# Probabilities transposed in half-height tiles, query blocks paired two apart, value products stacked

## The chip, the cores and the metric

The kernel runs on one core of a Trainium2 chip. The metric is the device time of one execution in microseconds. Three runs of the kernel before took 336.01, 339.49 and 340.27 us, so their median is 339.49 us; the profiled execution is a fourth one.

## The reference

Causal attention with a window of 128 keys and a slope per head (8 batches, 8 heads, 576 tokens, 64 numbers per head), and then a mixture of 8 experts in which each token goes to its best expert and each expert keeps its 80 tokens with the highest gate:

```
scores = scale * np.matmul(q, k.transpose(0, 1, 3, 2))
bias = slopes[:, None, None] * (-np.abs(rel).astype(np.float32))[None, :, :]
mask = (rel >= 0) & (rel < window)
scores = np.where(mask, scores + bias[None], -1000000000.0)
attn = softmax(scores)
x = np.matmul(attn, v)            # then (B, S, H * D): 4608 rows of 512
logits = x @ w_gate
expert_idx = np.argmax(logits, axis=1)
for e in range(E):
    tok_idx = the 80 tokens of expert e with the largest gate_w
    h = np.maximum(x[tok_idx] @ w1[e], 0.0)
    out[tok_idx] = gate_w[tok_idx, None] * (h @ w2[e])
```

All other rows of the output are zero.

## The kernel before

**The attention** takes some two thirds of the time. Queries are cut into 9 blocks of 64 rows (t = 0 to 8), heads into 4 pairs (g = 0 to 3). A block of queries sees three blocks of keys: its own (role 2) and the two before it (roles 1 and 0); for t = 0 the first two don't exist. A unit is a set of two neighbouring blocks of one pair of heads, (g, t) and (g, t+1), or two pairs at t = 8; there are 18 units in a batch. A cycle does two units, so a batch has 9 cycles and the whole attention 72. In each cycle TensorE does, in this order:

- `turned`, twice: the masked scores `e` of a unit (128 partitions: 2 blocks of 64 queries; 3 roles of 2 heads times 64 keys) are turned by three 128x128 transposes into a PSUM bank `pt`, and one `Exp` on ScalarE writes them as `ptb`, the keys of one head in partitions 0 to 63 and of the other in 64 to 127.
- `attend`, for each of two earlier units: 12 products `av<-v,ptb` (2 heads, 2 blocks, 3 roles) of 64 rows and 64 columns of weights with 73 moving columns (64 of v, 8 of gate logits and a one), each in a quadrant of the 128x128 array. The results of six units stand side by side in the two banks `av`; `attended` copies them into `xs` on ScalarE only after the sixth.
- `scores`, after each `attend`: 4 quadrant products `s<-kp,q` of 192 columns for the unit two cycles on. VectorE adds the bias and takes the row minimum (`e`, `mn`); GpSimd, for one of the four pieces ScalarE, subtracts it.

A float32 product in a quadrant is two records of TensorE in the trace, and a transpose is one; each has its own load of weights (PEld).

**Side work** goes between the scores of a cycle and the next cycle's transposes (`sides`): the gate logits of the values (`value_logits`: `s<-l_vt,wg`), their transposes into the columns of v (`value_columns`: `s<-ident,lxb` and the copies `v<-s` on VectorE), and the steps that merge each batch's best 80 tokens (`ttt`, `ts`, `at`).

**Order.** A planner records all operations of the attention with costs (`_cost`) and writes each engine's order out; `strict` keeps the three TensorE parts of a cycle in the order of the loop. Engines run in that order and wait on semaphores. SyncE issues the loads and stores in order; `transfers` says which go with which cycle, and a `None` in its lists is filled with one of the stores of zeros to the output (36 of 256 KB). Each is paced by a mark, a transpose's `Exp` or a score's reduction.

**The experts** follow the attention's merge: from 238 to 327 us, with weights that are loaded at the same time. The change does not touch them.

Of the kernel before, what the change touches and what calls it, by code (L numbers as in the profile page):

```python
# [29 lines left out]
class Plan:  # L30
# [107 lines left out]
    def add(self, ns_name, eng, name, args, kw):  # L138
# [12 lines left out]
        if name == "transpose":  # L151
            cols = 256.0 if outs[0].dtype == F32 else 128.0
        elif name == "matmul":
            cols = self._free(kw["rhs"]) * self._free(kw["lhsT"]) / P * (4 if kw["rhs"].dtype == F32 else 1)
# [8 lines left out]
        else:  # L163
# [4 lines left out]
            if name == "transpose" and not op.full:  # L168
                op.tiled = 2
# [61 lines left out]
    def pace(self, call, lead):  # L231
        call.leads.append(lead)
        call.op.deps.setdefault(lead.op, False)
# [152 lines left out]
def tile_attention_then_moe(  # L386
# [55 lines left out]
    def spare(i, k=0):  # L442
        return sps[i % 2][k][:, 128 if i < NUN and units[i][1][0][1] == 0 else 192:512]

# [18 lines left out]
    bn0 = const.tile([P, H, 128], F32, name="bn0")  # L463
# [11 lines left out]
    def make_bias(g):  # L475
        for h in (2 * g, 2 * g + 1):
            add_bias(bn0[:, h], h, ALL, rel0)
        for h in (2 * g, 2 * g + 1):
            add_bias(bneg[:, h], h, ALL, rel)
# [9 lines left out]
    kps = [persist.tile([P, 64 + S], F32, name=f"kp{i}") for i in range(NQ)]  # L489
    for rows in (LOW, HIGH):  # L490
        nc.gpsimd.iota(rel_i[rows], pattern=[[-1, 192]], base=WIN, channel_multiplier=1)
    nc.gpsimd.memset(kps[0][:, 0:64], 0.0)
# [3 lines left out]
    nc.vector.tensor_copy(rel0, rel[:, 64:192])  # L496
    nc.vector.memset(rel0[0:64, 0:64], FAR)
    make_bias(0)

    qs, v_t = {}, {}  # L500

    vts = [persist.tile([P, NP, NKB, VW], F32, name=f"v{i}") for i in range(2)]
    vtt = {}

    def load_v(b, g):
        w = NKB * VW
        return nc.sync.dma_start(
            out=vts[b % 2][:, g].rearrange("p n c -> p (n c)"), in_=v[b][:, w * g:w * g + w])
# [6 lines left out]
    def load_k(b, g, a=0, c=S):  # L515
        return nc.sync.dma_start(out=kps[(b * NP + g) % NQ][:, 64 + a:64 + c], in_=k[b, g, :, a:c])
# [6 lines left out]
    def load_pair(b, g):  # L523
        for a, c in ((0, 256), (256, S)) if b + g == 0 else ((0, S),):
            load_k(b, g, a, c)
            load_q(b, g, a, c)

    load_pair(0, 0)
    wg = const.tile([P, NP, 32], F32, name="wg")
    nc.sync.dma_start(out=wg.rearrange("p g c -> p (g c)"), in_=w_gate)  # L530
    for g in range(2):
        load_vt(0, g)
    load_pair(0, 1)
    for g in range(2):
        load_v(0, g)
    for g in range(2, NP):
        load_vt(0, g)
    load_pair(0, 2)
    load_pair(0, 3)
    for g in range(2, NP):  # L540
        load_v(0, g)
# [4 lines left out]
    for t in kps[1:]:  # L546
        nc.gpsimd.memset(t[:, 0:64], 0.0)
# [30 lines left out]

    def selection_constants():
# [19 lines left out]
        nc.gpsimd.iota(bi, pattern=[[S, B], [P, NU]], base=P, channel_multiplier=0)  # L599
# [83 lines left out]
    def lay(b, bank, gs, us, hh, par):  # L683
        rows, of = (LOW, HIGH)[hh], (LOW, HIGH)[par]
        u0, u1 = us
        lv = bank[:, 0:32 * (gs[1] - gs[0]) * (u1 - u0)].rearrange("p (u g c) -> p g u c", u=u1 - u0, c=32)
        k1 = min(2 * u1, NKB)
        nc.vector.tensor_copy(
            vts[b % 2][rows, gs[0]:gs[1], 2 * u0 + par:k1:2, D:VW],
            lv[of, :, 0:(k1 - 2 * u0 - par + 1) // 2, 9 * hh:9 * hh + 9])  # L690

    def value_columns(b, bank, us, gs=(0, NP)):
# [8 lines left out]
        for hh in range(2):  # L701
            for par in range(2):
                lay(b, bank, gs, us, hh, par)

    def blocks(g, t):
        return (g, t), (g, t + 1)

    BATCH = [blocks(g, t) for g in (0, 1) for t in (0, 2, 4)]
    BATCH += [blocks(g, 6) for g in range(NP)] + [((2 * u, 8), (2 * u + 1, 8)) for u in range(2)]
    BATCH += [blocks(g, t) for g in (2, 3) for t in (0, 2, 4)]  # L710
    NB = len(BATCH)
    NUN = B * NB
    units = [(i // NB, BATCH[i % NB]) for i in range(NUN)]
    es, pts, marks = {}, {}, {}

    def scores(i):
        b, st = units[i]
        (g, t), (g2, _) = st
        e = work.tile([P, 3, 2, 64], F32, tag="e", name=f"e{i}", bufs=6)
        mn = small.tile([P, 2], F32, tag="mneg", name=f"mn{i}", bufs=6)  # L720
        es[i] = e
        sp = sps[i % 2]
        o0 = 64 if t == 0 else 0
        n = 192 - o0
        with nc.together():
            for hh in range(2):
                for j, (gg, t_) in enumerate(st):
                    hs = slice(64 * hh, 64 * hh + 64)
                    nc.tensor.matmul(
                        sp[hh][64 * j:64 * j + 64, 0:n],  # L730
                        lhsT=qs[b, gg][hs, 64 * t_:64 * t_ + 64],
                        rhs=kps[(b * NP + gg) % NQ][hs, 64 * (t_ - 1) + o0:64 * (t_ - 1) + 192],
                        start=True, stop=True)
        yield
        for hh in range(2):
            bias = bnx[:, g // 2, hh] if g != g2 else bn0[:, 2 * g + hh] if t == 0 else bneg[:, 2 * g + hh]
            m = mn[:, hh:hh + 1]
            x = e[:, o0 // 64:, hh]
            marks["s", i] = nc.vector.tensor_tensor_reduce(
                x, sp[hh][:, 0:n].rearrange("p (k c) -> p k c", c=64),  # L740
# [636 lines left out]
```

## Time and profile before

| what | value |
|---|---|
| runs | 336.01, 339.49, 340.27 us; median 339.49 |
| profiled execution | 335.38 us, its span 333.6 us |
| TensorE busy, matrix products | 310.1 us, 93% of the span |
| VectorE, ScalarE, GpSimd busy | 56%, 45%, 39% |
| instructions | 16,416 |
| attention | from about 5 to 220 us |

The span is the time from the first to the last instruction; the execution's own time has 1.8 us around it. Busy shares are means over the whole span, and attention and experts differ: in the attention VectorE is above 80% and TensorE at 99%. A record of TensorE is as long as its data takes to go through, and records overlap, so what one costs is read from the distance between the starts of neighbours.

### The profile page before, as it was taken

What the parts mean: (1) busy time and instruction counts of PE and PEld (TensorE: products, weight loads), DVE (VectorE), ACT (ScalarE), POOL (GpSimd) and SP (SyncE); (2) the same over time, 40 slices, a digit from 0 to 9 for tenths busy, and PEclk for the clock granted to TensorE, in tenths of its full rate; (3) what the DMA queues carried; (4) which work ended last, traced back from release to release, by engine and by line L of the source; (5) the groups of instructions that cost most, each with busy time, mean ns of one, the idle gap of its engine ahead of it and who ended that gap; (6) DMA issues with size and microseconds to landing.
All of it is one profiled execution on the core that took longest, in us unless ns stands there. A gap on an engine that the chain in (4) does not pass through costs nothing. (4 is left out here: it accounts for less than half of the span.)

```text
span 333.6 us, 16416 instructions
## 1 busy us (share of the span) xinstructions
PE 310.1 (93%) x6727; PEld 226.4 (68%) x6727; DVE 187.2 (56%) x1005; ACT 151.1 (45%) x392; POOL 129.3 (39%) x351
## 2 busy tenths in 40 slices
PE   7998998999998999999899999998779999999992
PEld 5585766777776777777686787786675566655560
DVE  7665766787896797887697789775101011110000
ACT  8464555645654645655456556532003322223221
POOL 8543563464463455455346448400710111011111
PEclk9999999999999999999999999999759999999998
DMA  7989999999999899999889888971599999999300
GB/s 216 385 276 360 318 300 269 333 320 323 317 325 313 279 340 292 349 335 310 274 281 301 252 269 283 330 269 40 170 292 392 393 394 402 398 395 398 101 22 21
DMA packets 45131, 97.07 MB, mean 291 GB/s; under 512 B 4864, under 2 KB 5504, under 8 KB 45056
## 3 DMA queue, kind: packets, MB, share of 16 engines
q1 hardware_dynamic: 44032, 93.21, 81.5%
q0 software_dynamic: 1024, 2.81, 2.8%
q8 instruction: 53, 0.87, 1.1%
q14 instruction: 22, 0.18, 0.1%
HBM read 74.19 MB, written 21.81 MB: 288 GB/s over the span
## 5 line engine op out<-in xcount | busy, mean ns | idle before, releaser
L352 POOL TENSOR_SCALAR e<-e,mn 128x192 f32<-128x192 f32 (+1 forms) x216 | 88.0, 415 | 89.6 <-DVE mn L352 78.6
L352 PE MATMUL av<-v,ptb 64*64 64x73 f32 x3072 | 87.2, 228 | 5.4 <-issue 3.9
L352 ACT ACTIVATE ptb<-pt 128x256 f32<-128x256 f32 (+1 forms) x144 | 62.0, 463 | 59.5 <-PE pt L352 58.3
L352 PEld LDWEIGHTS av<-v,ptb 64*64 64x64 f32 x3072 | 73.2, 132 | 20.8 <-issue 15.6
L352 PE MATMUL s<-kp,q 64*64 64x192 f32 (+1 forms) x1152 | 78.2, 314 | 1.2 <-DVE mn L352 0.8
L352 DVE CUSTOM_DVE_ANT_0 e<-s,bneg 128x192 f32<-128x192 f32 x192 | 62.1, 352 | 30.2 <-PE s L352 27.5
L352 PE MATMUL pt<-ident,e 128*128 128x128 f32 x400 | 59.3, 281 | 1.5 <-POOL ij L352 0.8
L352 PEld LDWEIGHTS pt<-ident,e 128*128 128x128 f32 x400 | 43.1, 140 | 12.0 <-issue 3.7
L1328 DVE TENSOR_TENSOR ys<-ys,y 80x512 f32<-80x512 f32 x8 | 5.5, 684 | 80.5 <-ACT ys L1323 80.5
L1296 PEld LDWEIGHTS h<-xgTs,w 128*64 128x64 f32 x1024 | 39.6, 145 | 9.8 <-issue 9.3
L1296 PE MATMUL h<-xgTs,w 128*64 128x80 f32 x1024 | 41.4, 243 | 3.2 <-issue 2.7
L1321 PE MATMUL y<-w,hT 128*32 128x512 f32 (+1 forms) x288 | 42.8, 594 | 0.0
L352 PEld LDWEIGHTS s<-kp,q 64*64 64x64 f32 x1152 | 39.2, 132 | 3.6 <-issue 2.1
L352 ACT ACTIVATE e<-e,mn 128x192 f32<-128x192 f32 (+1 forms) x72 | 31.7, 440 | 18.3 <-DVE mn L352 18.3
L1272 POOL DMA_INDIRECT out_dram<-ys,sid x8 | 7.4, 920 | 79.0 <-ACT hT L1301 73.8
L352 ACT COPY xs<-av 128x438 f32<-128x438 f32 (+2 forms) x79 | 28.5, 401 | 15.2 <-PE av L352 14.2
L1321 PEld LDWEIGHTS y<-w,hT 128*32 128x32 f32 (+1 forms) x288 | 10.5, 105 | 25.0 <-issue 24.2
L352 DVE DVE_READ_ACCUMULATOR2_ANT mn<- 128x1 f32 x288 | 23.9, 83 | 0.0
L352 DVE TENSOR_SCALAR_CACHE_REDUCE ncm<-s 128x272 bf16<-128x272 f32 (+8 forms) x69 | 22.8, 380 | 1.3 <-PE s L352 1.3
L1301 ACT ACTIVATE hT<-h 128x320 f32<-128x320 f32 x16 | 7.0, 437 | 36.1 <-PE h L1296 36.1
L352 DVE CUSTOM_DVE_ANT_0 e<-s,bn 128x128 f32<-128x128 f32 x64 | 16.6, 289 | 12.0 <-PE s L352 10.2
L1321 PE MATMUL yx_d<-w,hT 128*32 128x512 f32 x32 | 15.2, 598 | 0.0
(149 smaller groups left out, 323.8 us busy)
## 6 DMA issues: line engine op xcount, KB each, us to landing
w<-in_moe_w_dram SPq DMA_DIRECT2D x48, 512.0 KB, 11.0
v<-in_v_dram SPq DMA_DIRECT2D x32, 328.5 KB, 4.8
x_dram<-xs SPq DMA_DIRECT2D x32, 292.0 KB, 4.8
l_vt<-in_vt_dram SPq DMA_DIRECT2D x32, 288.0 KB, 4.7
out_dram<-zero SPq DMA_DIRECT2D x36, 256.0 KB, 4.5
kp<-in_k_dram SPq DMA_DIRECT2D x31, 288.0 KB, 4.5
q<-in_q_dram SPq DMA_DIRECT2D x31, 288.0 KB, 4.8
w<-in_moe_w_dram SPq DMA_DIRECT2D x32, 256.0 KB, 4.2
```

What stands on the lines that cost most here:

```text
L352: c.ins = c.f(*c.args, **c.kw)
L1272: put = nc.gpsimd.indirect_dma_start(out=out, out_offset=bass.IndirectOffsetOnAxis(ap=sid[:, e:e + 1], axis=0), in_=ys, in_offset=None, bo ...
L1296: nc.tensor.matmul(hp[64 * hh:64 * hh + 64, R * fi:R * fi + R], lhsT=a[:, cc, f0:f0 + 64], rhs=xgT[:, cc], start=(cc == 0), stop=(cc == NC ...
L1301: relu = nc.scalar.activation(hT[:, 4 * f2:4 * f2 + 4].rearrange("p c r -> p (c r)"), hp[:, 0:4 * R], AF.Relu)
L1321: nc.tensor.matmul(o, lhsT=hT[:, f_, l0:l1], rhs=c[:, f_], start=st, stop=sp)
L1328: nc.vector.tensor_tensor(ys, ys, yp[0:R, 0:DM], ALU.add)
```

## The change

- **Pairs.** A cycle is written as a pair of two sets x = 0 and 1, and a set now holds blocks two apart, (g, t) and (g, t+2), or both pairs of heads at the same t, or blocks 0 and 1. The two sets of a pair mostly hold t and t+1, so that in the order (set, role) two neighbouring roles are two neighbouring key blocks, which a 128-row tile of v can hold.
- **Transposes.** `turned` does a whole cycle: for each head and each 128 columns of `e`, one transpose for rows 0 to 63 and one for rows 64 to 127, that is 12 of 64 rows of weights by 128 columns with 64 moving columns. The two row halves go to the two banks `pt`, alternating. There are still two `Exp` a cycle.
- **Products.** `attend` does a whole cycle: first 8 products with 128 rows of weights (two key blocks stacked) and 64 columns, then 8 quadrant products with 64 rows for the remaining block of each set (4 where only one set has one).
- **Copies.** The results stand in columns 0 to 145 of the two `av` banks in every cycle and are copied out in every cycle: 22 copies a batch in place of 8.
- **Transfers.** v is stored in HBM with 128 rows by all heads (five loads a batch, the last with 64 rows, for four, with the same bytes), x leaves in nine stores of 64 rows a batch in place of five of 128 or 64 (`SLOT` says which blocks share a tile). k and q are loaded earlier in the batch. The copies `v<-s` are six a batch in place of eight, and the columns of v are made in cycles 4 and 8 of the batch before.
- Ten `iota` in place of one, smaller first bias tables, and the planner's costs of half-height transposes.

```diff
@@ costs of the planner
-                return 109.0 if outs[0].dtype == F32 else 55.0
+                return 55.0 if outs[0].dtype != F32 else 109.0 if ins[0].shape[0] > 64 else 34.0
...
-            if name == "transpose" and not op.full:
+            if name == "transpose" and op.full and ins[0].shape[0] <= 64:
+                op.tiled, op.full = 1, False
+            elif name == "transpose" and not op.full:
                 op.tiled = 2
...
+    SLOT = ((3, 5), (2, 4), (6, 8), (0, 1), (7,))
...
+    def two(g, t):
+        return (g, t), (g, t + 2)
...
+    BATCH = [
+        (two(0, 2), two(0, 3)), (two(1, 2), two(1, 3)), (both(0, 0), both(0, 1)),
+        (two(0, 6), both(0, 7)), (two(1, 6), two(2, 3)), (two(2, 2), two(3, 3)),
+        (two(3, 2), both(2, 7)), (two(2, 6), first(2)), (two(3, 6), first(3)),
+    ]
...
+    def turned(c):
+        e = es.pop(c)
+        full, thirds = parts_of(c)
+        pt = work.tile([P, 2, 2, 3, 64], F32, tag="ptb", name=f"ptb{c}", bufs=2)
+        pts[c] = pt
+        i0 = 0 if full else 1
+        banks = [p_[:, 0:384].rearrange("p (h i q) -> p h i q", h=2, i=3) for p_ in ptp]
         with nc.together():
...
+            for hh in range(2):
+                cols = e[:, hh].rearrange("p x r c -> p (x r c)")
+                for i in range(i0, 3):
+                    w = 64 if i == 1 and not thirds else P
+                    for j, rows in enumerate((LOW, HIGH)):
+                        nc.tensor.transpose(
+                            banks[j][0:w, hh, i], cols[rows, P * i:P * i + w], ident[rows, rows])
+        for j in range(2):
+            marks["t", c, j] = nc.scalar.activation(
+                pt[:, j, :, i0:].rearrange("p h i q -> p h (i q)"),
+                banks[j][:, :, i0:].rearrange("p h i q -> p h (i q)"), AF.Exp)
...
+        with nc.together():
+            for x in range(0 if full else 1, 2):
                 for hh in range(2):
...
+                    for j, (g, t) in enumerate(pair[x]):
+                        product(x, hh, j, pt[:, j, hh, 2 * x], V[:, (t - 1) // 2 if t else 0, 2 * g + hh], hh == 0)
+        with nc.together():
+            for hh in range(2):
+                for j in range(2):
+                    for x in range(2 if thirds else 1):
+                        g, t = pair[x][j]
+                        rows, kb = (HIGH, t - 2) if x else (LOW, t)
+                        product(x, hh, j, pt[rows, j, hh, 1], V[rows, kb // 2, 2 * g + hh], not full and not x and hh == 0)
+        attended(c)
...
+            for of, u, rows, g in lot:
+                (nc.vector.tensor_copy if last and x else nc.scalar.copy)(
+                    xsb[b % 2][rows, u, 2 * g:2 * g + 2].rearrange("p h c -> p (h c)"), avp[x][of, 0:2 * VW])
...
+                2: vt_[0:1], 3: vt_[1:4], 4: [k_[0], q_[0], v_[0]], 5: [v_[1], k_[1], q_[1]],
+                6: v_[2:5], 7: [k_[2], q_[2], k_[3]],
...
     for c in range(1, NCY):
...
+        strict(turned, c)
...
+        strict(attend, c - 1)
+        if c + 2 < NCY:
+            scored(c + 2, 0)
...
+            scored(c + 2, 1, list(sides(c)))
...
-    for u in range(3):
+    for u in range(1, NU):
         store_x(LAST, u)
```

TensorE's order in the middle of the attention before, from the transposes of a full cycle to the second half of its scores (a row is a product or a transpose, `x2` are two of them; `pt_79` and `pt_80` are the banks of the transposes, `av_85` and `av_86` those of the value products):

```order
L352 MATMUL pt_79<-ident,e_493 128x128 x3
L352 MATMUL pt_80<-ident,e_496 128x128 x3
L352 MATMUL av_85<-v_97,ptb_498 64x73 x2
L352 MATMUL av_86<-v_97,ptb_498 64x73 x2
L352 MATMUL av_85<-v_97,ptb_498 64x73 x2
L352 MATMUL av_86<-v_97,ptb_498 64x73 x2
L352 MATMUL av_85<-v_97,ptb_498 64x73 x2
L352 MATMUL av_86<-v_97,ptb_498 64x73 x2
L352 MATMUL s_0_81<-kp_93,q_0_479 64x192 x2
L352 MATMUL s_1_82<-kp_93,q_0_479 64x192 x2
```

And a full cycle there now, from the last transposes to the first scores (in the rows `x4` eight stacked products, in the single ones the eight quadrants):

```order
L355 MATMUL pt_79<-ident,e_309 128x64
L355 MATMUL pt_80<-ident,e_309 128x64
L355 MATMUL av_85<-v_98,ptb_311 64x73 x4
L355 MATMUL av_86<-v_98,ptb_311 64x73 x4
L355 MATMUL av_85<-v_98,ptb_311 64x73
L355 MATMUL av_86<-v_98,ptb_311 64x73
...
L355 MATMUL s_0_81<-kp_93,q_0_298 64x192 x2
L355 MATMUL s_1_82<-kp_93,q_0_298 64x192 x2
L355 MATMUL s_0_83<-kp_93,q_0_298 64x192 x2
L355 MATMUL s_1_84<-kp_93,q_0_298 64x192 x2
```

The two stretches of products of a cycle now stand one behind the other with two tile shapes, and the transposes alternate between the banks.

ScalarE's order in two cycles of the middle before (`ptb<-pt` are the exponentials, `e<-e,mn` the fourth piece's subtraction):

```order
L352 ACTIVATE ptb_475<-pt_79 128x384
L352 ACTIVATE ptb_476<-pt_80 128x384
L352 ACTIVATE e_472<-e_472,mn_473 128x3x64
L352 ACTIVATE e_480<-e_480,mn_481 128x3x64
L352 ACTIVATE ptb_484<-pt_79 128x384
L352 ACTIVATE ptb_485<-pt_80 128x384
```

And two cycles now:

```order
L355 ACTIVATE ptb_369<-pt_79 128x384
L355 ACTIVATE e_366<-e_366,mn_367 128x192
L355 ACTIVATE ptb_369<-pt_80 128x384
L355 COPY xs_125<-av_85 128x146
L355 COPY xs_125<-av_86 128x146
L355 ACTIVATE ptb_373<-pt_79 128x384
L355 ACTIVATE e_371<-e_371,mn_372 128x192
L355 ACTIVATE ptb_373<-pt_80 128x384
L355 COPY xs_125<-av_85 128x146
L355 COPY xs_125<-av_86 128x146
```

Two copies have come into each cycle, behind its second exponential.

SyncE's order in the first batch before, from the last first loads to the next batch's gate inputs `l_vt_154`:

```order
L352 DMA v_97<-in_v_dram 128x657 x2
L352 DMA out_dram<-zero 128x512
L352 DMA l_vt_154<-in_vt_dram 128x576
L352 DMA out_dram<-zero 128x512 x3
L352 DMA l_vt_154<-in_vt_dram 128x576
L352 DMA out_dram<-zero 128x512
L352 DMA l_vt_154<-in_vt_dram 128x576 x2
```

And now, with `l_vt_143` for the same inputs:

```order
L355 DMA kp_96<-in_k_dram 128x576
L355 DMA q_3_104<-in_q_dram 128x576
L355 DMA out_dram<-zero 128x512 x10
L355 DMA l_vt_143<-in_vt_dram 128x576
L355 DMA out_dram<-zero 128x512 x2
L355 DMA l_vt_143<-in_vt_dram 128x576 x3
```

Twelve stores of zeros, in place of five, stand ahead of the last three loads of `l_vt`.

## Rows read from the trace of the kernel before

**Rows 1.** Page, busy time of each engine (share of the span) and instructions.
```profile
PE 310.1 (93%) x6727; PEld 226.4 (68%) x6727; DVE 187.2 (56%) x1005; ACT 151.1 (45%) x392; POOL 129.3 (39%) x351
```

**Rows 2.** Windows: length, busy us (instructions) by engine, granted clock, DMA share, GB/s.
```profile
60.00:80.00 20.00, 19.83 (x507) 15.38 (x506) 16.57 (x90) 10.78 (x27) 10.36 (x29) 1.00 0.96 324
```

**Rows 3.** Waits of TensorE and its loads: us in total, times, longest.
```profile
PE av L352 <- issue: 3.9, 7, 1.5
...
PEld av L352 <- ACT xs L352: 2.4, 9, 0.3
```

**Rows 4.** Timeline of TensorE's products in one cycle: start, length of the stretch.
```profile
17.34 0.32 PE L352 MATMUL s<-kp,q 64*64 64x192 f32 x1
...
17.48 0.50 PE L352 MATMUL s<-kp,q 64*64 64x192 f32 x6
17.91 0.51 PE L352 MATMUL s<-ident,lxb 64*128 64x64 f32 x5
18.35 0.87 PE L352 MATMUL pt<-ident,e 128*128 128x128 f32 x6
19.16 0.61 PE L352 MATMUL av<-v,ptb 64*64 64x73 f32 x24
19.59 0.51 PE L352 MATMUL s<-kp,q 64*64 64x192 f32 x8
19.91 0.56 PE L352 MATMUL av<-v,ptb 64*64 64x73 f32 x24
20.30 0.50 PE L352 MATMUL s<-kp,q 64*64 64x192 f32 x8
20.73 0.88 PE L352 MATMUL pt<-ident,e 128*128 128x128 f32 x6
```

**Rows 5.** The av banks' instructions: duration in ns, least, median, most; first and last start.
```profile
L352 PE MATMUL av<-v,ptb x3072: 220/223/276, 13.1 to 220.2; 64*64 64x73 f32 x192
L352 PE MATMUL av<-ident,lxb x5: 216/222/273, 11.4 to 11.7; 64*128 64x64 f32 x4, 64*64 64x64 f32 x1
```

**Rows 6.** Timeline of TensorE among the experts.
```profile
254.78 0.60 PE L1321 MATMUL y<-w,hT 128*32 128x512 f32 x3
...
255.21 0.60 PE L1321 MATMUL y<-w,hT 128*32 128x512 f32 x3
...
255.75 4.65 PE L1296 MATMUL h<-xgTs,w 128*64 128x80 f32 x128
260.33 0.49 PE L1254 MATMUL xgT<-ident,xn 80*128 80x80 f32 x4
```

**Rows 7.** ScalarE's groups from 60 to 200 us: busy us, mean ns.
```profile
L352 ACT ACTIVATE ptb<-pt 128x384 f32<-128x384 f32 x74 | 34.6, 487 | 30.5 <-PE pt L352 29.4
L352 ACT ACTIVATE e<-e,mn 128x192 f32<-128x192 f32 x37 | 16.7, 453 | 6.4 <-DVE mn L352 6.4
L352 ACT COPY xs<-av 128x438 f32<-128x438 f32 x22 | 10.5, 529 | 4.7 <-PE av L352 4.1
L352 ACT COPY xs<-av 64x146 f32<-64x146 f32 x20 | 5.5, 276 | 0.1
L352 ACT COPY xs<-av 128x292 f32<-128x292 f32 x10 | 4.0, 404 | 3.0 <-PE av L352 2.8
```

**Rows 8.** Timeline of TensorE in the first batch, with a stall.
```profile
26.87 0.30 PE L352 MATMUL av<-v,ptb 64*64 64x73 f32 x7
28.63 0.49 PE L352 MATMUL av<-v,ptb 64*64 64x73 f32 x17 [1.46 <-issue]
28.93 0.51 PE L352 MATMUL s<-kp,q 64*64 64x192 f32 x8
29.37 0.45 PE L352 MATMUL s<-l_vt,wg 128*32 128x288 f32 x4
```

**Rows 9.** Timeline of SyncE's queue: start and length of issues.
```profile
17.21 1.68 SPq L352 DMA_DIRECT2D out_dram<-zero  x3
...
21.41 0.87 SPq L352 DMA_DIRECT2D l_vt<-in_vt_dram  x2
```

**Rows 10.** Windows of the first batch, columns as in Rows 2.
```profile
14.00:16.00 2.00, 2.00 (x36) 1.00 (x29) 1.19 (x7) 0.23 (x1) 0.83 (x2) 1.00 1.03 391
16.00:18.00 2.00, 2.00 (x58) 1.54 (x57) 1.67 (x8) 1.21 (x3) 0.53 (x2) 1.00 0.72 247
22.00:24.00 2.00, 2.00 (x68) 1.55 (x60) 1.16 (x8) 0.94 (x3) 1.02 (x3) 1.00 0.94 239
```

**Rows 11.** DMA issues: KB of each, median us from issue to landing.
```profile
l_vt<-in_vt_dram SPq DMA_DIRECT2D x32, 288.0 KB, 4.7
out_dram<-zero SPq DMA_DIRECT2D x36, 256.0 KB, 4.5
```

More of the change, by code (lines that the diff above doesn't have):

```diff
@@ L598, in selection_constants @@
         bi = const.tile([P, B, NU], I32, name="bi")
-        nc.gpsimd.iota(bi, pattern=[[S, B], [P, NU]], base=P, channel_multiplier=0)
+        for j, rows in enumerate((LOW, HIGH)):
+            for u in range(NU):
+                at_ = SLOT[u][min(j, len(SLOT[u]) - 1)] - j
+                nc.gpsimd.iota(bi[rows, :, u], pattern=[[S, B]], base=P + 64 * at_, channel_multiplier=0)
         nc.vector.tensor_copy(idc[:, :, 0], bi.rearrange("p b u -> p (b u)"))
@@ L700, in value_columns @@
         yield
[L701 to L724, printed above, removed]
+        for u0, u1, rw in ((us[0], min(us[1], NU - 1), ALL), (NU - 1, us[1], LOW)):
+            for hh in range(2 if u0 < u1 else 0):
+                lv = bank[rw, n * (u0 - us[0]):n * (u1 - us[0])].rearrange("p (u g c) -> p u g c", u=u1 - u0, c=32)
+                nc.vector.tensor_copy(
+                    vts[b % 2][rw, u0:u1, 2 * gs[0] + hh:2 * gs[1]:2, D:VW], lv[:, :, :, 9 * hh:9 * hh + 9])
@@ new lines, in tile_attention_then_moe, with scores @@
+    units = [tuple(first_role(x, st) for x, st in enumerate(p_)) for p_ in BATCH]
+    units = [(c // CB, units[c % CB], BATCH[c % CB]) for c in range(NCY)]
+    es, mns, pts, marks = {}, {}, {}, {}
+    def scores(c, x):
+        b, r0, st = units[c][0], units[c][1][x], units[c][2][x]
+        if x == 0:
+            es[c] = work.tile([P, 2, 2, 3, 64], F32, tag="e", name=f"e{c}", bufs=3)
+            mns[c] = small.tile([P, 2, 2], F32, tag="mneg", name=f"mn{c}", bufs=3)
+        e, mn, sp = es[c], mns[c], sps[x]
+        n = 192 - 64 * r0
@@ L742, in scores @@
-            if hh == 0 or i % 2 == 0:
-                nc.gpsimd.tensor_scalar(x, x, -1.0, m, ALU.mult, ALU.add)
-            else:
-                nc.scalar.activation(x, x, AF.Identity, bias=m, scale=-1.0)
-    def turned(i):
-        e = es.pop(i)
-        r0 = 1 if units[i][1][0][1] == 0 else 0
-        pp = ptp[i % 2]
-        with nc.together():
-            for r in range(r0, 3):
-                nc.tensor.transpose(pp[:, P * r:P * r + P], e[:, r].rearrange("p h c -> p (h c)"), ident)
-        pt = work.tile([P, 3, P], F32, tag="ptb", name=f"ptb{i}", bufs=4)
-        pts[i] = pt
-        marks["t", i] = nc.scalar.activation(
-            pt[:, r0:3].rearrange("p r c -> p (r c)"), pp[:, P * r0:3 * P], AF.Exp)
@@ L763, in attend, with product @@
+    def attend(c):
+        b, _, pair = units[c]
+        pt, V = pts.pop(c), vts[b % 2]
+        full, thirds = parts_of(c)
+        def product(x, hh, j, lhsT, rhs, start):
+            w = VW * hh
+            nc.tensor.matmul(
+                avp[x][64 * j:64 * j + 64, w:w + VW], lhsT=lhsT, rhs=rhs, start=start, stop=True,
+                skip_group_check=True)
         with nc.together():
-            for n, role in enumerate((2, 1, 0)):
+            for x in range(0 if full else 1, 2):
@@ new lines, in attend, with attended @@
+        with nc.together():
[6 more added lines that the diff above has]
+        attended(c)
+    def attended(c):
+        b, _, pair = units[c]
+        last = b == LAST and c % CB == CB - 1
+        for x, st in enumerate(pair):
+            to = [[(u, h) for u in range(NU) for h, t_ in enumerate(SLOT[u]) if t_ == t][0] for _, t in st]
+            lot = [(ALL, to[0][0], ALL, st[0][0])]
+            if to != [(to[0][0], 0), (to[0][0], 1)] or st[0][0] != st[1][0]:
+                lot = [((LOW, HIGH)[j], u, (LOW, HIGH)[h], st[j][0]) for j, (u, h) in enumerate(to)]
+            for of, u, rows, g in lot:
+                (nc.vector.tensor_copy if last and x else nc.scalar.copy)(
+                    xsb[b % 2][rows, u, 2 * g:2 * g + 2].rearrange("p h c -> p (h c)"), avp[x][of, 0:2 * VW])
@@ L1047, in whole, with scored @@
             pass
-    def scored(i, side=()):
-        g = scores(i)
+    def scored(c, x, side=()):
+        g = scores(c, x)
         strict(next, g)
```

263 lines of the change are left out of this document (119 added, 144 removed).

## The prediction, made before the changed kernel was run

> **What bounds the kernel now.** I read the busy times first: TensorE's products take 93% of the span, no other engine more than 56% [rows 1]. A mean hides stages, so the next view is the windows of the attention: from 60 to 80 us TensorE is busy 19.83 of 20 us, VectorE 16.6, ScalarE 10.8, and the DMA engines 96% [rows 2]. Then the waits: TensorE's own largest is for "issue", time in which no semaphore held it, and for ScalarE's copies of the value products its weight loads wait 2.4 us in nine places [rows 3]. So in the attention TensorE works without a gap, and the time is the sum of the distances between starts of its products. VectorE and the transfers come next and have little left. The experts are untouched and I count them at nothing.
>
> A quiet cycle shows where the 2.38 us from one stretch of transposes to the next go [rows 4]: transposes and the change to products 0.81 (18.35 to 19.16), products 0.43, scores 0.32, products 0.39, scores and the change back 0.43.
>
> **The price of a change of tile shape.** The same eight score records take 0.32 us when quadrant products follow and 0.43 when 128x128 transposes do, so the change costs 0.11. In front of half-height tiles it is no cheaper: a score record is 0.32 long, so the last of the stretch at 17.48 starts at 17.66, and the first `lxb` transpose, of 64 rows and 128 columns, starts 0.25 later; the last score at 20.30 starts at 20.48, and the full transpose also 0.25 later [rows 4]. Among the experts, with all 128 rows in use on both sides, four products `y` take 0.43 and the step to `h`, from 32 to 64 columns of weights, 0.54: again 0.11 [rows 6]. I take 0.10 for a change (0.09 to 0.11), and 0.05 more for the first step of a stretch, which the two stretches of products show (0.43 after a change, 0.39 without one).
>
> [...]
>
> **Transposes.** Six full ones with their change take 0.81, so 0.71 without it. Now there are twelve of 64 rows. Their step stands in the `lxb` stretch: 0.51 long, its last record 0.22 [rows 4, 5], so 0.29 for four steps of which the first has 0.05 extra: 0.06 each. Those five lie in one row half, one behind the other. The new ones alternate between the halves. Do the halves run side by side? Quadrant products do: 24 records in 0.39 is four in 0.063 [rows 4], and these four load 4 times 64 columns of weights meanwhile, twice what one half-height transpose loads in its 0.06. I take that two transposes of different halves share one step: 0.05 + 6 x 0.062 = 0.42, a gain of 0.29 in a full cycle. If they don't, it is 0.05 + 12 x 0.062 = 0.80, a loss of 0.08.
>
> [...]
>
> **Products.** Before, 12 groups of four quadrant records, 0.82 with their two first steps. Now 8 pairs of stacked records and 4 groups of quadrants. A pair of 128 rows by 64 columns is in the experts' `h`: 128 records from 255.75 to 260.33, less 0.15 for its first step and the change behind it, is 0.069 a pair for 80 columns [rows 6], so 0.063 for 73. A pair costs what a group of quadrants does, therefore stacking halves the instructions of these products but saves no time: 12 steps before, 12 now. What it adds is a change of shape between stacked and quadrant products, with a first step: 0.55 + 0.10 + 0.30.
>
> **Scores** keep 0.65 and the change of 0.11 ahead of the transposes.
>
> A full cycle is then 0.42 + 0.09 + 0.55 + 0.09 + 0.30 + 0.65 + 0.11, in finer figures 2.233 against 2.374: -0.14. Per batch, before: 9 cycles less 0.41 in four units with first blocks (one transpose, three groups, 64 score columns twice), 19.74. Now six full cycles, two whose scores are 0.11 shorter, and one with first blocks on both sides (a third of the transposes, half the stacked products and half the score columns less: 1.53): 19.18. That is -0.56 a batch and **-4.5 us** in eight.
>
> **Side work.** The full-height `lxb` transposes stood ahead of full transposes and shared their shape. In two cycles a batch they now stand ahead of half-height ones: a change and a first step more, 0.15 x 2 x 7 = **+2.1** (0 to 2.2). The merge steps' products are of other shapes before and after.
>
> **Instructions.** A full cycle has 16 + 16 + 12 + 16 records where there were 48 + 6 + 16, about 10% fewer. TensorE's "issue" waits, like the one ahead of 28.63 [rows 8], come to 3.9 us at the value products alone [rows 3]; I let a fifth of that go: **-0.8** (0 to -3).
>
> **First batch.** SyncE has twelve stores of zeros ahead of the last three `l_vt` loads in place of five. Seven more of 256 KB are 1.83 MB: at 391 GB/s 4.7 us, at 239 GB/s 7.7 [rows 10]. In the window 16 to 18 the DMA engines had 0.28 x 2 = 0.6 us free. Before, the last `l_vt` was issued by 22.28 [rows 9] and landed some 4.7 later [rows 11], at 27.0, and the products that read it came at 29.37 [rows 8]: 2.4 of slack. So TensorE would wait 1.7 to 4.7 us at `value_logits` of batch 1, and all its later work behind it in order; if transfers overtake each other, nothing. I take **+2.5** (0 to 5), near the low end because the queue is fullest at the higher rate.
>
> **ScalarE.** Copies a batch go from 8 to 22. One of 64x146 takes 276 ns, one of 128x292 404 [rows 7]; a copy of 128x146 isn't there, and I take 0.28. In a cycle: two exponentials 0.97, a subtraction 0.45, two copies 0.55, together 1.98 of at least 2.23. The copies may run from the end of a cycle's quadrant products to the next stacked ones, that is during scores, change, transposes, change: 1.27 us plus side work. Two copies and the subtraction are 1.0, so they hide, and I count nothing. In three cycles a batch there are three or four copies, 1.28 to 1.55 with the subtraction: up to 0.3 x 3 x 8 = 7 us where no side work stands, so 0 to 4 as a bound.
>
> **The rest**, at nothing: the `iota` and bias tables run on GpSimd and VectorE while TensorE has its first work, VectorE does two copies `v<-s` fewer a batch; nine stores of x in place of five are SyncE issues of 0.4 us in a queue that is paced, not full. The last copy of `av` gets shorter by two thirds: **-0.3**.
>
> Sum: -4.5 + 2.1 - 0.8 + 2.5 - 0.3 = -1.0, so 334.4 against the profiled 335.38. That execution is the shortest of the four; their mean is 337.8. I put the changed kernel's median at **337 us**. 2% of the median, 6.8 us, is about what a measurement of this kernel can tell from no change.
>
> **Rivals.**
> (1) The products wait for ScalarE (slower). In its order each cycle's second exponential stands behind the subtraction, and the copies behind that. If the second exponential starts only once VectorE has done the scores that the subtraction needs, then exponential, subtraction and copies together, 0.49 + 0.45 + 0.55 = 1.49, have to fit in the 1.27 us in front of the stacked products. It decides where a cycle's side work is under 0.2 us. Price 0.22 x 72 = 16 us at most, half with side work in every other cycle: 345 to 353, say **348**. For it: the nine waits of `av` for copies even with eight a batch [rows 3]. Against: ScalarE is busy 10.8 of 20 us [rows 2] and would be some 16.
> (2) The row halves don't run side by side: 0.37 more a full cycle, in about 70 cycles +26, **363**. For it: the only half-height transposes in the trace are in one half, so nothing shows it. Against: the quadrants. [...]
> (3) A change between shapes that both have 64 rows is free after all, or TensorE's issue waits shrink with its instructions: 0.11 x 71 = -7.8, **329**. Against: the 0.25 at 17.91.
> (4) The change doesn't do what it says: VectorE or the transfers, at 83% and 96% [rows 2], set the pace as soon as TensorE is shorter, and the gain is nil: 335.4 + 2.5, within the forecast's range.
>
> **How the numbers follow.** Forecast, with (4): 0.57, its own range 330 to 343. Rival (1) 0.17, (2) 0.08, (3) 0.18. Faster by over 2% (under 332.7): rival (3) and a sliver, 0.20. Slower by over 2% (over 346.3): (2), most of (1) and the upper end of the ScalarE and first-batch terms, 0.24. The range leaves out (2) and the ends: 328 to 350.
>
> **What would show it.** Twelve transposes in 0.42 from first to last step, starts in pairs; 0.2 between the last transpose and the first stacked product, the same between stacked and quadrant; a quiet full cycle of 2.23; a TensorE wait of 2 to 3 us at `s<-l_vt,wg` near 30 us; few waits of `av` for `xs`. Wrong it is if transposes step singly by 0.06, if `av` waits for copies in most cycles, or if the cycles stretch beyond the sum while TensorE waits for `e` of VectorE and GpSimd.

## The result, and the profile after

The changed kernel takes 324.62 us (median of 323.5, 323.94, 325.3 and 332.82) where the kernel before, beside it, takes 338.13: a ratio of 0.959, with a 95% interval of 0.949 to 0.968. On a second chip the ratio was 0.962 (0.957 to 0.968), 318.4 against 330.9. Ratios, here and below, are of fast executions alone, without the slow ones such as that of 332.82. So the change makes the kernel faster by 4%; the prediction was 337 with a range of 328 to 350.

The profiled execution took 323.5 us, with a span of 321.7 in place of 333.6. The page's first part answers to [rows 1]:

```profile
PE 302.0 (94%) x6135; PEld 219.5 (68%) x6135; DVE 173.4 (54%) x991; ACT 158.9 (49%) x486; POOL 128.4 (40%) x356
```

The window of the attention answers to [rows 2]:

```profile
60.00:80.00 20.00, 20.00 (x473) 15.09 (x462) 15.74 (x92) 13.30 (x44) 10.98 (x30) 1.00 0.94 313
```

TensorE is as full as before, so the time is still the sum of its steps; it has 592 products and transposes fewer. The waits of TensorE and of its loads, which answer to [rows 3] (us in total, times, longest):

```profile
PE av L355 <- DVE v L355: 5.9, 1, 5.9
...
PE av L355 <- issue: 1.2, 2, 0.9
...
PE s L355 <- issue: 0.5, 1, 0.5
...
PE pt L355 <- issue: 0.2, 1, 0.2
...
PEld av L355 <- ACT xs L355: 0.4, 2, 0.3
```

[rows 3] has the kernel before's stalls at the value products alone. Its scores and transposes had these, so that it lost 7.4 us in all:

```profile
PE s L352 <- issue: 3.0, 5, 1.3
...
PE pt L352 <- issue: 0.5, 1, 0.5
```

Three things are to be seen: one new wait of 5.9 us, issue stalls of the attention that have gone from 7.4 to 1.9 us, and waits for copies that have gone from 2.4 us to 0.4 although there are more copies. TensorE's timeline of one cycle with its side work, which answers to [rows 4]:

```profile
129.55 0.58 PE L355 MATMUL pt<-ident,e 64*128 64x64 f32 x12
130.06 1.15 PE L355 MATMUL av<-v,ptb 128*64 128x73 f32 x32
131.03 0.72 PE L355 MATMUL s<-kp,q 64*64 64x192 f32 x16
131.68 0.44 PE L355 MATMUL s<-ttt,sst 32*128 32x320 bf16 x3
```

Transposes and change take 0.51 (0.81 before), products with their inner change 0.97 (0.82 before), scores with the change behind them 0.65. These are scores of which half have 128 columns (the row gives the form of the first); where all have 192 columns they take 0.76 (117.15 to 117.91). A full cycle without side work runs from 42.36 to 44.62, that is 2.26, nearly as the prediction had it (2.233).

Where the 11.9 us of span come from, by the starts of the same stretches in both traces: up to the transposes that open batch 1 the changed kernel is 4.8 us later (40.44 against 35.65). From there to the last value product it takes 169.5 us in place of 184.5, 15.0 less. These are the windows of that stretch, before and now; the second number is TensorE's busy time, so it stood idle for 6.8 us before and for 2.0 now:

```profile
35.65:220.16 184.51, 177.70 (x4478) 137.19 (x4477) 145.11 (x821) 101.87 (x272) 93.93 (x254) 1.00 0.93 305
```

```profile
40.44:209.97 169.53, 167.52 (x3933) 128.57 (x3933) 133.15 (x808) 109.03 (x356) 92.81 (x254) 1.00 0.96 316
```

The merge behind it takes the same 18.3. The experts take 1.7 less, which is not the change's: that stage took 95.2 and 93.5 us in the first profiles of the two kernels, in which the granted clock stood at 0.50 for 10.3 and 5.8 us of it, and 88.1 (before) and 87.7 and 87.7 (changed) in three later profiles, in which it was 1.00 there but for the last few us. The attention alone tells the kernels apart.

The 4.8 us of the first batch are not the wait of 5.9 us alone. The pages' rows of the granted clock (40 slices of some 8 us, in tenths of full speed), before and now:

```profile
PEclk9999999999999999999999999999759999999998
```

```profile
PEclk9969999999999999999999999996679999999998
```

While TensorE waited, the granted clock fell from 1.00 to 0.50, and it stayed there from 15.6 to 22.4 us. The first products and scores behind the wait took 3.15 us (17.97 to 21.12); the same ones took 1.73 in a run in which the clock stayed at 1.00 (the loads of v ahead, below).

### The profile page after: what moved, and what is told of

Its sections match the earlier page's. It is cut to its first block, busy times and chain, and to the rows that moved or that the text cites. A ratio compares the mean times of both kernels' runs of the same rounds, so it can differ in the third digit from the quotient of the medians.

```text
span 321.7 us, 15170 instructions
## 1 busy us (share of the span) xinstructions
PE 302.0 (94%) x6135; PEld 219.5 (68%) x6135; DVE 173.4 (54%) x991; ACT 158.9 (49%) x486; POOL 128.4 (40%) x356
## 5 line engine op out<-in xcount | busy, mean ns | idle before, releaser
L355 POOL TENSOR_SCALAR e<-e,mn 128x192 f32<-128x192 f32 (+2 forms) x216 | 86.9, 415 | 82.1 <-DVE mn L355 72.1
L355 ACT ACTIVATE ptb<-pt 128x384 f32<-128x384 f32 x144 | 65.3, 474 | 60.4 <-PE pt L355 59.8
L355 PE MATMUL av<-v,ptb 128*64 128x73 f32 (+1 forms) x2048 | 82.2, 237 | 7.2 <-DVE v L355 5.9
L355 DVE CUSTOM_DVE_ANT_0 e<-s,bneg 128x192 f32<-128x192 f32 x192 | 60.0, 351 | 40.2 <-PE s L355 26.4
L355 PEld LDWEIGHTS av<-v,ptb 128*64 128x64 f32 (+1 forms) x2048 | 64.9, 136 | 18.7 <-DVE v L355 6.0
L355 PE MATMUL s<-kp,q 64*64 64x192 f32 (+2 forms) x1152 | 60.6, 314 | 0.5 <-issue 0.5
L355 ACT COPY xs<-av 128x146 f32<-128x146 f32 (+1 forms) x175 | 42.4, 283 | 11.8 <-PE av L355 10.9
L355 PE MATMUL pt<-ident,e 64*128 64x64 f32 (+1 forms) x832 | 41.8, 230 | 0.4 <-POOL e L355 0.2
L355 PEld LDWEIGHTS pt<-ident,e 64*128 64x128 f32 (+1 forms) x832 | 31.7, 135 | 12.6 <-issue 6.1
L355 DVE CUSTOM_DVE_ANT_0 e<-s,bnx 128x192 f32<-128x192 f32 (+2 forms) x64 | 17.3, 301 | 8.0 <-ACT ptb L355 5.4
```

Source lines behind the costliest of these rows:

```text
L355: c.ins = c.f(*c.args, **c.kw)
```

## The experiments

**Transposes undone.** One part is taken back, everything else stays:

```diff
-                    for j, rows in enumerate((LOW, HIGH)):
-                        nc.tensor.transpose(
-                            banks[j][0:w, hh, i], cols[rows, P * i:P * i + w], ident[rows, rows])
+                    nc.tensor.transpose(ptp[hh][0:w, P * i:P * i + P], cols[:, P * i:P * i + w], ident)
```

> The changed kernel with its transposes undone: six of 128x128 a cycle in place of twelve of 64 rows, everything else as in the changed kernel. Theory: the transposes are where the gain is; a full cycle loses 0.29 us again, 20 us in 70 cycles, and the merge steps pay again for a change of shape (0.12 us twice a batch, 2 us), less 0.15 us twice a batch for the transposes of the gate logits (2 us): about 344, slower than the kernel before. Rival: the gain came from elsewhere (fewer stalls, earlier loads) and the transposes in half height give under half of it: 335 or less.

332.97 us, a ratio to the kernel before of 1.002 (0.998 to 1.006). All of the gain is gone, where the rival had under half of it, and the price is some 14 us instead of 20. (The time itself lies under the rival's 335, but the kernel before takes 333.04 us on this chip, 5 us less than beside the first runs.) The timeline of the same cycle as above:

```profile
136.78 0.87 PE L355 MATMUL pt<-ident,e 128*128 128x128 f32 x6
137.59 1.15 PE L355 MATMUL av<-v,ptb 128*64 128x73 f32 x32
138.56 0.72 PE L355 MATMUL s<-kp,q 64*64 64x192 f32 x16
139.21 0.44 PE L355 MATMUL s<-ttt,sst 32*128 32x320 bf16 x3
```

The transposes take their 0.81 again, 0.30 more, as expected. Three batches in the middle (batches 4 to 6) take 79.3 us where the changed kernel takes 72.5, 2.3 a batch, which is 18 in eight. Up to 3 us come back, since this kernel, with 5,719 products and transposes, has no issue stall among the waits of its attention, where three profiles of the changed kernel have 0 to 3.0 us; the rest of the difference to 14 is open.

**The halves apart.** The same twelve transposes, in another order:

```diff
-            for hh in range(2):
-                cols = e[:, hh].rearrange("p x r c -> p (x r c)")
-                for i in range(i0, 3):
-                    w = 64 if i == 1 and not thirds else P
-                    for j, rows in enumerate((LOW, HIGH)):
+            for j, rows in enumerate((LOW, HIGH)):
+                for hh in range(2):
+                    cols = e[:, hh].rearrange("p x r c -> p (x r c)")
+                    for i in range(i0, 3):
+                        w = 64 if i == 1 and not thirds else P
```

> The changed kernel with the six transposes of the lower row half first and the six of the upper behind them, in place of alternating. Theory: two halves run side by side only where neighbours in TensorE's order lie in different halves, so the step is 0.062 for each transpose; 0.05 + 12 x 0.062 = 0.80 for a full cycle in place of 0.42, some 0.37 x 65 = 24 us more than the changed kernel, a ratio to the kernel before of about 1.03. Rival: TensorE takes the loads and transposes of the other half ahead, whatever the order in the program: under 5 us more.

326.15 us, a ratio of 0.984 (0.977 to 0.990) where the changed kernel beside it has 0.962: some 7 us. Both forecasts are missed. The timeline:

```profile
132.73 0.76 PE L355 MATMUL pt<-ident,e 64*128 64x64 f32 x12
133.42 1.15 PE L355 MATMUL av<-v,ptb 128*64 128x73 f32 x32
```

The stretch takes 0.69 to the first product, between 0.51 (alternating) and the 0.90 of twelve single steps with the change. The starts in the trace show three of the second half's six transposes within 0.01 us of one of the first half's (the first of them at 132.91), and the other three alone; in the changed kernel all twelve start in pairs. So the halves do run side by side, and the alternating order is worth 0.18 us a cycle. A batch without stalls takes 25.43 us (115.63 to 141.06) in place of 24.15, 1.3 more, which is 10 in eight.

**The products unstacked.** Each stacked product becomes two quadrant products, so the shape does not change among them. Each row half has its own bank:

```diff
+            for half in (0, 1):
+                for hh in range(2):
+                    for j in range(2):
+                        for x in range(0 if full else 1, 2):
+                            g, t = pair[x][j]
+                            product(
+                                x, hh, j, (LOW, HIGH)[x ^ half], pt[:, j, hh, 2 * x],
+                                V[:, (t - 1) // 2 if t else 0, 2 * g + hh], hh == 0 and (half == 0 or not full))
```

> The changed kernel with each stacked value product as two quadrant products of 64 rows, so that the products of a cycle have one shape (24 products, 48 records, in place of 16 and 32); each row half has its own bank, and the sum of the two banks is left out of the copies (only one is copied), so the output lacks a part. Theory (the sum of the prediction): 12 steps as before but no change of shape among the products, 0.16 us less in a full cycle, some 9 to 11 us less in all: 313 to 315. Rival: TensorE's issue stalls grow with the number of its instructions (some 7,160 products in place of 6,135, where the kernel before had 6,727 and lost 6.1 us to such stalls from 30 to 218 us and the changed kernel 1.9 us): 5 us or more of stalls come back, 317 to 321.

345.02 us, a ratio of 1.026 (1.017 to 1.036): slower than the kernel before, by some 2 to 4%. (The profiled execution took 350.8 us at a granted clock of 0.926 in the mean; in its attention the clock fell to 0.50 from 54.7 to 61.5 and from 78.6 to 82.0 us, during a stall of 2.7 us and behind one of 1.7, so the totals of this profile are high.) The timeline of one cycle and TensorE's waits:

```profile
141.17 0.59 PE L355 MATMUL pt<-ident,e 64*128 64x64 f32 x12
141.69 1.00 PE L355 MATMUL av<-v,ptb 64*64 64x73 f32 x48
142.51 0.81 PE L355 MATMUL s<-kp,q 64*64 64x192 f32 x16
```

```profile
PE av L355 <- issue: 12.1, 13, 2.0
PE s L355 <- issue: 6.3, 6, 2.6
...
PE pt L355 <- issue: 4.3, 2, 2.7
```

The products did what the sum says: they take 0.82 in place of 0.97, 0.15 less. (In this cycle the scores behind them give half of it back, 0.74 where the changed kernel has 0.66 in the same cycle, 128.46 to 129.12.) But 22.7 us of issue stalls came with the 7,223 products and transposes, and more than the saving is gone. The rival was right in kind, and its 317 to 321 us far too low.

What these stalls go with shows in the traces' records of transfers. Of the two queues that each page calls `instruction`, q8 brings 16 KB at a time. For the changed kernel, the kernel before and the unstacked one (transfers, MB, share of the DMA engines):

```profile
q8 instruction: 48, 0.79, 1.0%
```

```profile
q8 instruction: 53, 0.87, 1.1%
```

```profile
q8 instruction: 57, 0.93, 1.2%
```

That is one transfer for every 127 to 128 of TensorE's products and transposes in each of the three. In the attention of the unstacked kernel such a transfer lands every 5 us, and all 21 stalls end 1.1 to 1.6 us behind a landing. So do the 13 of the kernel before and the 4 of the changed one, and those of all other profiles here, 79 in all; the "issue" waits later in the kernel, among the experts, do not (3.8 us or more behind one). I read the stalls of the attention as TensorE waiting for its instructions; no run isolates that. The transfers just ahead of a stall's end take no longer than the others (1.0 us in the median), so by this reading they come late because they start late; why some do is open.

**Less data beside it.** The same kernel, whose 36 stores of zeros write 8 of 512 columns:

```diff
-        fill.append(lambda c=c: nc.sync.dma_start(out=out[P * c:P * (c + 1)], in_=zero[:, 0:DM]))
+        fill.append(lambda c=c: nc.sync.dma_start(out=out[P * c:P * (c + 1), 0:8], in_=zero[:, 0:8]))
```

> The kernel of e2b_unstacked (stacked products as quadrant products, sum of the halves left out), and the 36 stores of zeros to the output write 8 of 512 columns, so 9.3 of 97 MB less move, the most of it during the attention. e2b_unstacked lost 22.7 us to issue stalls of TensorE. Theory: TensorE outruns the transfers that bring its instructions, and these queue among the data, so with less data the stalls fall by a third or more, to 15 us or less. Rival: they come from the number of instructions alone, however busy the DMA engines are: 19 us or more.

335.66 us, a ratio of 1.012 (1.007 to 1.016), and 16.5 us of issue stalls:

```profile
PE av L355 <- issue: 7.9, 13, 1.3
PE s L355 <- issue: 7.9, 8, 1.2
...
PE pt L355 <- issue: 0.7, 1, 0.7
```

Between both forecasts (15 or less, 19 or more). With one profile of each, and one of them at a lower clock, it doesn't settle how far busy transfers lengthen a stall. The theory's first half agrees with the landings above (all 22 stalls here end 1.2 to 1.6 us behind one), which do not isolate it; its second half, that the transfers queue among the data, has nothing for it: they take 0.99 us in the median in place of 1.00. That 16.5 us remain with a tenth of the data gone speaks for the number of instructions as the larger cause.

**Both kernels again,** to see whether the stalls of the first two profiles were luck.

> The kernel before as it is, for a second profile. Theory: its issue stalls of TensorE in the attention go by the number of its instructions and come again, 5 us or more from 30 to 218 us, and the waits of its value products for the copies again some 2 us; the attention ends 12 to 17 us later than in the changed kernel, and the stage of the experts is as long as in the changed kernel on the same chip. Rival: the stalls of the first profile were luck, and here they are under 3 us.

330.41 us (one run). Issue stalls of 9.5 us and again eight waits of weight loads for copies:

```profile
PE av L352 <- issue: 6.4, 7, 1.2
PE s L352 <- issue: 3.1, 3, 2.4
...
PEld av L352 <- ACT xs L352: 2.2, 8, 0.3
```

> The changed kernel as it is, on the chip of the runs below, as their base. Theory: its gain over the kernel before is the same on another chip, a ratio of 0.955 to 0.965, and its issue stalls of TensorE from 30 to 207 us are again 1 to 3 us, since they go by the number of its instructions. Rival: the low stalls of its first profile were luck: 5 us or more here.

318.4 us, a ratio of 0.962. No issue stall of TensorE among the waits of its attention, only the long one:

```profile
PE av L355 <- DVE v L355: 5.4, 1, 5.4
```

> The changed kernel as it is, once more beside the kernel before. Theory: issue stalls under 2.5 us from 30 us to the end of the attention, waits of the value products for copies under 0.5 us. Rival: its stalls are as many as the kernel before's.

320.43 us (one run), with 3.0 us of issue stalls, over the 2.5 that I had allowed, and 0.2 us of waits for copies. The attention's last product starts at 212.91 us in it, and at 222.37 in the kernel before on the same chip: 9.5 us apart, under the 12 to 17 forecast, where the profile of the changed kernel ahead of it, from another chip, has 208.21, 14 us apart. The issue stalls in the attention of all profiles, by TensorE's products and transposes in the whole kernel: 5,719, none; 6,135, from none to 3.0 in seven profiles (three of the changed kernel, two with the loads of v ahead, one with the halves apart and one with copies twice); 6,727, 7.4 (its rows `av`, `s` and `pt`) and 9.5; 7,223, 16.5 and 22.7. The rival of luck falls.

**Copies twice.** Each copy out of PSUM is issued two times on ScalarE:

```diff
+                for _ in range(1 if last and x else 2):
```

> The changed kernel with every copy of value products out of PSUM issued twice on ScalarE (22 more copies of 0.28 us a batch). Theory: ScalarE has slack, since copies and one subtraction, 1.1 + 0.45, come near the 1.27 us and the side work between a cycle's products and the next ones only in cycles with little side work: 0 to 5 us more, 324 to 330. Rival (the first of the prediction): the exponentials count too and ScalarE is close to the bound, so nearly all 0.56 us show in most cycles: over 345.

326.91 us, a ratio of 0.986 (0.977 to 0.996), some 8 us above the changed kernel's ratio of 0.962. That is over the 5 us that the theory allowed (by the ratios; the two kernels ran on different chips), and far under the rival. ScalarE is busy 17.3 of 20 us, the products wait for copies 3.9 us in ten places, and their weight loads 6.3 us where they waited 0.4 in the changed kernel (a window of the attention, and the rows of the waits):

```profile
60.00:80.00 20.00, 19.60 (x467) 14.90 (x458) 14.91 (x96) 17.27 (x59) 10.96 (x30) 1.00 0.99 329
```

```profile
PE av L355 <- ACT xs L355: 3.9, 10, 0.7
...
PEld av L355 <- ACT xs L355: 6.3, 14, 0.9
```

So two copies a cycle are hidden, and four are not quite.

**The loads of v ahead.** The new wait of 5.9 us stands in two timelines of the changed kernel, TensorE's and VectorE's:

```profile
11.56 0.52 PE L355 MATMUL pt<-ident,e 64*128 64x64 f32 x10 [0.25 <-POOL e L355]
17.97 1.94 PE L355 MATMUL av<-v,ptb 128*64 128x73 f32 x32 [5.88 <-DVE v L355]
```

```profile
17.01 0.37 DVE L355 COPY v<-av 128x72 f32<-128x72 f32 x2 [3.65 <-DMA v<-in_v_dram]
17.66 0.25 DVE L355 COPY v<-av 64x18 f32<-64x18 f32 x2 [0.28 <-DMA v<-in_v_dram]
```

The first products wait for the copies into the columns of v, and these for v's last loads, which stand behind other loads in SyncE's queue. Before, a load held one pair of heads, and the first products needed two of four loads; now a load holds 128 keys of all heads, and the copies need all five. The experiment moves the last two ahead:

```diff
-    for i in range(3):
+    for i in range(NPR):
         load_v(0, i)
     load_pair(0, 0, 384, S)
     load_vt(0, 2)
     load_vt(0, 3)
     load_pair(0, 2)
-    load_v(0, 3)
-    load_v(0, 4)
```

> The changed kernel with the two last loads of v of batch 0 moved ahead, behind its first three. Theory: the changed kernel's one long wait of TensorE (5.9 us, value products waiting for the copies into the columns of v, which wait for the last load of v) comes from the new layout of v, in which a product needs tiles that hold all heads; with the loads ahead the wait shrinks to under 1 us and the time is 5 to 6 us less than the changed kernel's 323.5 to 325.3, about 318.5. Rival A: the gate inputs of batch 1 are then late instead (the wait forecast for the first batch), giving 2 to 4 us back: 320 to 322. Rival B: the transfers at the start are bound by bytes, so another load that has moved back stops TensorE for as long: no change.

316.56 us, a ratio of 0.951 (0.940 to 0.962). The wait is 1.5 us, and batch 1 begins at 35.13 in place of 40.44 us. That is more than the wait shrank by: the first value product starts 4.0 us sooner (13.94), and with the shorter wait the granted clock stays at 1.00 there, which saves 1.4 us in the first products and scores (13.94 to 15.67). Of rival A there is 0.9 us, at the gate inputs of the first batch. Beside the changed kernel on one chip:

> The changed kernel with the last two loads of v ahead (as e1_v_first), beside the changed kernel on the same chip. Theory: the long wait for the columns of v shrinks from 5.9 to 1.5 us and nothing else moves, so it is 4 to 5.5 us below the changed kernel, a ratio to the kernel before lower by 0.013 to 0.017. Rival: a wait of the same size comes back later in the first two batches: less than 2 us below.

316.86 us against 318.4, ratios of 0.956 (0.951 to 0.962) and 0.962 (0.957 to 0.968): 1.5 us by the medians, with intervals that overlap, so the theory's 4 to 5.5 is missed. The profiles show how: batch 1 begins 2.7 us sooner (36.64 against 39.36) and batch 2 3.5 us sooner, but the last product only 1.7 us (206.49 against 208.21). The wait is 2.1 us here, and the clock was at 0.50 for 3.4 us behind it, from 14.5 us on.

```profile
PE av L355 <- DVE v L355: 2.1, 1, 2.1
PE xgT L1282 <- issue: 1.8, 1, 1.8
...
PE s L355 <- issue: 0.9, 1, 0.9
```

The time came out as the rival's, less than 2 us below, but not by its cause: no wait of that size came back in the first two batches. What was won there was partly lost later, among others to issue stalls, which vary from run to run by as much. It has the lowest medians of all kernels here, but these runs don't settle whether it is faster than the changed kernel.

## Why the prediction was wrong

The forecast was -1.0 us; the profile has -11.9, the medians -13.5.

**What bounds the kernel** was right in the main: TensorE's steps, in both kernels. That it works "without a gap" was read from one window, 60 to 80 us; from batch 1 to the last value product it stood idle 6.8 of 184.5 us.

**Transposes, products and the price of a change** were right to 0.03 us. In a full cycle the transposes and their change were to take 0.51 and take 0.51, the products 0.94 and take 0.97. Unstacking showed the change and first step at 0.15 (0.97 to 0.82). Rival (2) falls: the halves run side by side, the twelve starts in six pairs (129.55 to 129.91).

**The sum per batch** failed: "-0.56 a batch" with +0.27 of side work, so -0.29, where a batch without stalls went from 25.24 (115.44 to 141.16, less a stall of 0.48 in the scores that start at 122.96) to 24.17 (113.22 to 137.39): -1.07. The windows of the two batches:

```profile
115.44:141.16 25.72, 25.46 (x645) 1.00 0.97 322
```

```profile
113.22:137.39 24.17, 24.17 (x569) 1.00 0.98 325
```

Summed over that batch, transposes fell by 2.18 (2.28 forecast), products and scores together rose by 1.19 from 13.74 (by the terms of the forecast 1.72 from 12.95, which is its 19.74 less 6.79 for transposes with their change; so its new sum was 0.26 short too), and side work fell by 0.07 (a rise of 0.27 forecast). Three terms were mis-sized:
- *Products before.* Of the 0.79 us that they and the scores took more than I had, 0.33 is a wait for copies in the eighth cycle of the batch, which [rows 3] had as 2.4 us in nine places and which I used for a rival, but never as something the change removes. Some 0.24 is the discount of "three groups" for first blocks: a half cycle with half of its products takes 0.58 (140.19 to 140.77) where one with all takes 0.71 (131.95 to 132.66), so 0.13 is saved four times a batch, where "three groups" are 0.19. I read it as products in half the quadrants, where leaving out half of them saves less than half of the steps; no experiment isolates it, and the rest is open.
- *ScalarE.* The first rival had the wrong sign. Waits for copies fell from 2.4 to 0.4 us, although the copies rose from 10 to 22 a batch (the kernel before has 80 in its trace, so ten and not the eight of its description). The reading, argued and not isolated: copies of 0.28 us each cycle let the banks go sooner than a burst of two copies of 0.53 every third cycle.
- *Side work.* "The merge steps' products are of other shapes before and after" was wrong for those that end in products of 64 rows. Before, a change followed them; in front of half-height transposes none shows. The last merge product of one such cycle, before:

```profile
120.75 0.46 PE L352 MATMUL s<-ts,ob 128*80 128x54 bf16 x5
121.14 0.87 PE L352 MATMUL pt<-ident,e 128*128 128x128 f32 x6
```

and after:

```profile
118.24 0.46 PE L355 MATMUL s<-ts,ob 128*80 128x54 bf16 x5
118.49 0.45 PE L355 MATMUL pt<-ident,e 64*64 64x64 f32 x8
```

The same five products take 0.39 before and 0.25 now. That is won in two cycles a batch, and pays for the two changes that the `lxb` transposes add.

**Instructions**, "a fifth of that", -0.8 with -3 as its end: measured 7.4 to 1.9 us in the first pair of profiles, -5.5, and more in the later ones. This is the term that failed most clearly. It was taken from the 3.9 us at the value products alone, not from all 7.4, and I treated the stalls as a share of the instructions, where a tenth fewer (6,135 for 6,727) removed most of them. By the reading above they are waits for the transfers of q8, and they were the more, the sooner 128 products and transposes, about as many as there are to a transfer, were done: without stalls these last some 6.5 us in the kernel with full transposes, 5.4 in the changed kernel and 5.0 in the kernel before. It also turns the reading of the stacking: by steps alone stacked products cost up to 0.15 us a cycle, 10 us in all, and the unstacked kernel is slower by more than that, for the stalls.

**First batch**, +2.5 at the gate inputs of batch 1: the end of that batch is 4.8 us later, but by a wait of 5.9 us at the columns of v and by the lower clock that came with it (1.4 us in the first products and scores), less a stall of 1.5 that the kernel before had there and shorter steps. The wait comes from a layout whose dependence I had not followed: the description of the change says of v's loads only that the bytes are the same. The forecast wait doesn't show behind it: no wait for the gate inputs of batch 1 is among TensorE's waits.

Together: +4.8 in the first batch and -15.0 in the seven behind it, where TensorE's idle time fell by 4.8, nearly all of it stalls, and its busy time by 10.2. Of that, the steps of the batch above make 1.07 x 7 = 7.5, of which some 2 are waits for copies; the other 2.7 isn't attributed, and stalls too short for the table of waits, like the 0.48 above, are in it. The experts' -1.7 goes with the clock. Rivals (1), (2) and (4) fall. The time came out near rival (3), by its second half: issue waits that shrink with the instructions, with the shape changes still priced as forecast. It was given 0.18. Its 329 was worked out from its first half, so that it lies near is luck.

## What to carry to other kernels

Where an engine is full, add up its steps from the distances between starts, but then check the sum against a whole period of the trace before taking differences: here the sum of the old kernel was 0.79 us a batch short and that of the new one 0.26, and the difference alone, 0.53 in eight batches, is 4 of the 11 us by which the forecast missed. Count instructions as a cost of their own: with TensorE full of small products, issue stalls went from none to over 16 us as its products and transposes rose by a quarter, and in the attention each ended 1.1 to 1.6 us behind the landing of a transfer of the queue that the page calls q8 `instruction`. When a layout is changed, follow which loads the first use needs, not the bytes.

## What the runs showed of the hardware

- Issue stalls grew steeply with TensorE's products and transposes over the same work: none at 5,719, up to 3.0 us at 6,135, 7.4 to 9.5 at 6,727, 16.5 to 22.7 at 7,223. All 79 of them in the attention ended 1.1 to 1.6 us behind the landing of a 16 KB transfer of the instruction queue q8, of which there was one for every 127 to 128 products and transposes.
- During the wait of 5.9 us in the first batch the granted clock fell to 0.50, and the products and scores behind it took 3.15 us in place of 1.73.
- Half-height transposes of the two row halves shared their steps when they alternated (0.51 us for twelve with the change behind them), and only partly when each half stood in a row (0.69).
- The same five merge products, the last with 64 rows and 80 columns of weights, took 0.25 us to the start of half-height transposes behind them and 0.39 to that of full ones.
